# w2's last 96 rows as 32-row matmuls for eight token tiles at a time, in a fused attention and SwiGLU kernel

## The chip, the cores and the metric

The kernel runs on one core of one Trainium2 chip. The metric is the device time of one execution in microseconds, as the median of several runs. A core has the engines TensorE (matmuls, and a separate stream of weight loads), VectorE, ScalarE, GpSimd (called POOL in the profile) and SyncE (SP), which issues the transfers. The hardware profiler records one execution, instruction by instruction; that record is the trace, and its summary the profile.

## The reference

The input x has 2048 tokens of 512 elements (S = 2048, D = 512), all in bf16. The output mixes two branches token by token:

```
g = sigmoid(sum(x * gate_w))                # one number per token
a = linear_attention(x, wqkv) @ wo          # 32 heads of 16; phi(t) = elu(t) + 1 + 1e-6
b = (silu(x @ w1) * (x @ w3)) @ w2          # F = 1376 hidden columns
out = g * a + (1 - g) * b
```

In the attention, o = (phi(q) @ kv) / (phi(q) . z + 1e-6) with kv = sum over tokens of phi(k)^T v and z = sum of phi(k). There is no softmax, so kv, and its product with wo, are small matrices computed once.

F = 1376 is 10 x 128 + 96. The ten full slices of 128 hidden columns and the 96 that remain are handled apart; the change is about the 96.

## The kernel before

The tokens are 16 tiles of 128 (t), four tiles make a block (tb, 512 tokens). PSUM, where matmuls write, has eight banks of 128 x 512 fp32. The schedule is written out by hand: each engine runs its instructions in the order in which the program emits them, and all transfers of the main part go through SP's queue in order.

The first part (until about 47 us) loads x and the weights, projects q and k for each tile (L177), applies phi (L190 to L195), sums phi(k) on POOL (L209) and accumulates x^T phi(k) in banks 0 to 3 (L225).

The second part is a loop over the four blocks (L481). For each block, ten GLU steps (glu_step, L267) run: each makes a 128 x 512 piece of the hidden layer, already transposed (hidden columns on partitions, tokens along the row), with four matmuls for w1 (L272), four for w3 (L278), the silu on ScalarE (L283) and the product on VectorE (L284), into `hT[tb]`. These matmuls write banks 4 to 7 in rotation (`mm_tile`). In block 0, further steps stand between the GLU steps: kv_step after step 2 and m2_step after step 4 (L410, L426), which make the small attention matrix M2 with tiled matmuls (128 x 32 and 32 x 32 of the array), den_step (L316: the denominators on VectorE and POOL, the scaled q, and its transposing transfer to `pqT`), and rem_step.

rem_step(tb) (L231) handles the 96 remaining hidden columns and the gate for the four tiles of a block. Sixteen matmuls of 193 columns (L239: 96 of w1, 96 of w3, one of gate_w) give token-major results; silu, tanh and product follow (L245, L246, L249), the product goes into `hrem` (four tiles of 96 columns, padded to 128 with zeros that POOL wrote at the start, L92), `g_all` and `omg_all` get g and 1 - g (L254, L258), and a transposing transfer puts it behind the ten slices in `hT[tb][:, FC, :]` (L262).

After the ten GLU steps of a block, four output steps (out_step, L441) run, one for each tile. Each makes the attention part with four matmuls (L447), scales it by g on ScalarE into `aga` (L452), makes the GLU part with eleven matmuls, ten of 128 rows and one of 96 (L460), and on VectorE multiplies it by 1 - g, adds aga and writes `o` (L464), which is stored (L477). Both results use banks 0 to 3 in rotation (`ab_tile`). The last tile's GLU part is made in three column pieces (256, 128 and 128 columns), each of eleven matmuls. Between the output steps stand rem_step of the next block (after the second) and den_step for the next block's tiles (after each). The 96 rows of w2 are loaded by a transfer of their own, the last of the weight loads (L153).

Of the kernel before, what the change touches and what calls it, by code (L numbers as in the profile page):

```python
# [16 lines left out]
def kernel(  # L17
# [17 lines left out]
    nc = tc.nc  # L35
    P = nc.NUM_PARTITIONS

    Bb, S, D = A_x.shape
    F = B_w1.shape[1]
# [3 lines left out]
    NT = S // P  # L43
    TB = 512
    NTB = S // TB
    TPB = TB // P
    FC = F // P
    FR = F - FC * P
    F0 = FC * P
    HPC = P // Dh  # L50
    ZP = 4
    NR = 2 * FR + 1
    RP = 32
    RB = P // RP
    HPR = RP // Dh

    x2d = A_x.flatten_outer_dims()
    out2d = out.flatten_outer_dims()
# [5 lines left out]
    consts = ctx.enter_context(tc.tile_pool(name="consts", bufs=1))  # L64
    work = ctx.enter_context(tc.tile_pool(name="work", bufs=2))
# [12 lines left out]
        out=bmask[:], in_=bmask[:], pattern=[[-Dh, HPC], [0, Dh]], compare_op=ALU.is_ge,  # L78
# [15 lines left out]
    zaccb = consts.tile([P, D], BF16, name="zaccb")  # L94
    zb = consts.tile([P, D], BF16, name="zb")
# [18 lines left out]
    w2 = consts.tile([P, FC + 1, D], BF16, name="w2")  # L114
# [38 lines left out]
    dq.dma_start(out=w2[:FR, FC, :], in_=B_w2[F0:F, :])  # L153
# [76 lines left out]

    def rem_step(tb):  # L231

        hr = hrem[tb % 2]
        for half in range(2):
            ps = mm_tile()[:].rearrange("p (j n) -> p j n", j=2)
            for j in range(2):
                t = tb * TPB + half * 2 + j
                for kc in range(KC):
                    nc.tensor.matmul(  # L239
                        ps[:, j, 0:NR], lhsT=xT[:, kc, t * P : (t + 1) * P],  # L240
                        rhs=wr[:, kc, 0:NR], start=(kc == 0), stop=(kc == KC - 1),
                    )
# [3 lines left out]
            nc.scalar.activation(  # L246
                out=th_all[:, t0 : t0 + 2], in_=ps[:, :, 2 * FR], func=ACT.Tanh, scale=0.5
            )
            nc.vector.tensor_tensor(  # L249
                out=hr[:, half * 2 : half * 2 + 2, 0:FR], in0=ps[:, :, FR : 2 * FR],  # L250
                in1=sg[:], op=ALU.mult,
            )
# [5 lines left out]
        nc.vector.tensor_scalar(  # L258
            out=omg_all[:, tl], in0=th_all[:, tl], scalar1=-0.5, scalar2=0.5,
            op0=ALU.mult, op1=ALU.add,  # L260
        )
# [42 lines left out]
    def den_scale(t):  # L304
# [5 lines left out]
                :, :, :, :, None  # L310
            ].to_broadcast([P, KC, RB, HPR, Dh]),
            op=ALU.mult,
# [9 lines left out]


    hT = {}
    hT[0] = work.tile([P, FC + 1, TB], BF16, tag="hT", name="hT")
# [84 lines left out]
    def kv_step():  # L410
        kv_ps = ab_tile()[:, 0 : KC * RP].rearrange("p (c q) -> p c q", q=RP)
        for c in range(KC):
            for kc in range(KC):
                for g in range(RB):
                    fs = slice(c * P + g * RP, c * P + (g + 1) * RP)
                    nc.tensor.matmul(  # L416
# [9 lines left out]
    def m2_step():  # L426
        ps = [ab_tile() for _ in range(RB)]
        for c in range(KC):
            for g in range(RB):
                rows = slice(g * RP, (g + 1) * RP)  # L430
# [7 lines left out]
            else:  # L438
                nc.vector.tensor_copy(out=M2[:, g, :], in_=ps[g][:])

    def out_step(tb, tt):  # L441
        t = tb * TPB + tt
        ts = slice(t * P, (t + 1) * P)
        tl = slice(tt * P, (tt + 1) * P)
        a_ps = ab_tile()
        for c in range(KC):
            nc.tensor.matmul(  # L447
                a_ps[:], lhsT=pqT[:, c, ts], rhs=M2[:, c, :],
                start=(c == 0), stop=(c == KC - 1),
            )  # L450
        aga = work.tile([P, D], FP32, tag="aga", name="aga")
        nc.scalar.activation(out=aga[:], in_=a_ps[:], func=ACT.Copy, scale=g_all[:, t : t + 1])  # L452
        o = work.tile([P, D], BF16, tag="o", bufs=3, name="o")
        last = t == NT - 1
        for lo, w in ((0, 2 * P), (2 * P, P), (3 * P, P)) if last else ((0, D),):
            cs = slice(lo, lo + w)
            b_ps = ab_tile()
            for fc in range(FC + 1):
                n = P if fc < FC else FR
                nc.tensor.matmul(  # L460
                    b_ps[:, 0:w], lhsT=hT[tb][:n, fc, tl], rhs=w2[:n, fc, cs],
                    start=(fc == 0), stop=(fc == FC),
                )
            nc.vector.scalar_tensor_tensor(  # L464
                out=o[:, cs], in0=b_ps[:, 0:w], scalar=omg_all[:, t : t + 1], in1=aga[:, cs],
                op0=ALU.mult, op1=ALU.add,
            )
            if t < 2:
                rows = out2d[0 : 2 * P, :].rearrange("(p j) d -> p j d", j=2)[:, t, :]
            else:  # L470
                rows = out2d[ts, :]
            if last and w == P:

                if lo + w < D:
                    continue
                cs = slice(2 * P, D)
            dq.dma_start(out=rows[:, cs], in_=o[:, cs])  # L477

    z_step()
    den_at = {5: 0, 6: 1, 8: 2, 9: 3}  # L480
    for tb in range(NTB):  # L481
        for fc in range(FC):
            glu_step(tb, fc)
            if tb == 0:
                if fc in den_at:
                    den_step(den_at[fc])
                if fc == 2:
                    kv_step()
                if fc == 4:
                    m2_step()  # L490
                    z_order()
                    den_products(0)
                if fc == 7:
                    rem_step(0)
        for tt in range(TPB):
            out_step(tb, tt)
            if tb + 1 < NTB:
                if tt == 0:
                    hT[tb + 1] = work.tile([P, FC + 1, TB], BF16, tag="hT", name="hT")
# [33 lines left out]
```

## Time and profile before

| | |
|---|---|
| median of 3 runs | 178.66 us (178.36 to 179.07) |
| the profiled execution | 179.09 us, span 177.4 us |
| granted TensorE clock | 0.999 of full |
| TensorE matmuls, busy | 172.9 us, 97% of the span, 922 recorded |
| TensorE weight loads, busy | 83.5 us, 47% |
| VectorE, busy | 101.0 us, 57% |
| ScalarE, busy | 62.1 us, 35% |
| POOL, busy | 64.2 us, 36% |
| HBM read / written | 8.56 MB / 2.10 MB |

The span runs from the first to the last instruction of the profiled execution; its time is a little longer. In the profile, PE is TensorE's matmuls and PEld its weight loads, DVE is VectorE, ACT is ScalarE. A row of a group gives the line of the kernel, the engine, the operation, what is written and read, the shape and the count, then the busy time of the group in us, the mean duration of one in ns, and the idle time of the engine just before them with what ended it. A row of the timeline or of the chain gives the start and the length of a stretch in us. Matmuls overlap in their pipeline, so the busy time of a group isn't the count times the mean. Some records of matmuls can be missing, so a count can be short of the program's by a few.

### The profile page before, as it was taken

Reading aid. Unit: us, or ns where it says so; the run is one execution under the profiler, and the core shown is the slowest. Engines: PE = TensorE matmul, PEld = TensorE weight load, DVE = VectorE, ACT = ScalarE, POOL = GpSimd, SP = SyncE. Lnnn points to the kernel's source line nnn. Section 1 sums busy time; section 2 is a strip of 40 time slices with the busy share of each in tenths; the row PEclk is TensorE's granted clock in tenths of the full one; section 3 lists DMA queues with packets and bytes.
Section 4 is the critical chain, followed back from the end, with each engine's and each line's share of the span. In section 5 each row is a group of like instructions: output and inputs, shape, how many; then the busy total and the mean of one; then the engine's idle time right before and its main releaser. Section 6 shows DMA issues by size and latency. Waiting matters only on the chain.

```text
span 177.4 us, 2610 instructions
## 1 busy us (share of the span) xinstructions
PE 172.9 (97%) x922; PEld 83.5 (47%) x939; DVE 101.0 (57%) x195; ACT 62.1 (35%) x113; POOL 64.2 (36%) x108
## 2 busy tenths in 40 slices
PE   8999999999999999999999999999999999999993
PEld 5444444444444464644444464444445444444453
DVE  0299798888774988675434266634325664433222
ACT  3255444544644441332342223143322223342130
POOL 7077666567301867746200044540004432000000
PEclk9999999999999999999999999999999999999999
DMA  5998949994103022343100013510000332000001
GB/s 170 273 206 227 190 76 316 395 350 123 33 1 33 0 59 59 80 94 96 30 0 0 0 44 81 104 45 0 0 4 30 89 89 59 0 0 4 30 30 59
DMA packets 29724, 15.41 MB, mean 87 GB/s; under 512 B 21552, under 2 KB 28048, under 8 KB 29712
## 3 DMA queue, kind: packets, MB, share of 16 engines
q1 hardware_dynamic: 29440, 15.25, 34.3%
q8 instruction: 7, 0.11, 0.3%
q10 hardware_dynamic: 272, 0.01, 0.1%
q14 instruction: 5, 0.04, 0.1%
HBM read 8.56 MB, written 2.10 MB: 60 GB/s over the span
## 4 chain that ended last, share of the span: by engine, by line
PE 97%; issue 1%; DVE 0%
PE bank L460 21%; PE bank L278 20%; PE bank L272 19%; PE bank L177 16%; PE bank L225 8%; PE bank L447 8%; PE bank L239 3%; PE bank L328 2%; PE bank L334 1%; PE bank L416 0%; PE bank L431 0%; DVE o L464 0%
## 5 line engine op out<-in xcount | busy, mean ns | idle before, releaser
L284 DVE TENSOR_TENSOR hT<-bank,sg 128x512 bf16<-128x512 f32 x40 | 27.3, 682 | 32.4 <-PE bank L278 31.4
L278 PE MATMUL bank<-xT,w 128*128 128x512 bf16 x158 | 40.8, 379 | 0.2
L272 PE MATMUL bank<-xT,w 128*128 128x512 bf16 x156 | 40.5, 379 | 0.2
L460 PE MATMUL bank<-w,hT 128*128 128x512 bf16 (+3 forms) x194 | 40.5, 355 | 0.2
L283 ACT ACTIVATE sg<-bank 128x512 bf16<-128x512 f32 x40 | 23.9, 597 | 46.1 <-PE bank L272 43.8
L306 POOL TENSOR_TENSOR pqs<-pq,rden 128x512 bf16<-128x512 bf16 x16 | 16.9, 1057 | 55.1 <-issue 48.2
L177 PE MATMUL bank<-wqk,xT 128*128 128x512 bf16 x126 | 31.0, 387 | 0.1
L460 PEld LDWEIGHTS <-hT 128*128 128x128 bf16 (+1 forms) x198 | 18.5, 98 | 19.8
L209 POOL TENSOR_TENSOR zacc<-zacc,pk 128x128 f32<-128x128 f32 x56 | 23.3, 447 | 10.4 <-DVE pk L195 10.4
L464 DVE SCALAR_TENSOR_TENSOR o<-bank,omg_all,aga 128x512 bf16<-128x512 f32 (+2 forms) x18 | 12.4, 692 | 25.6 <-PE bank L460 25.5
L278 PEld LDWEIGHTS <-w 128*128 128x128 bf16 x160 | 15.6, 98 | 18.9
L272 PEld LDWEIGHTS <-w 128*128 128x128 bf16 x160 | 15.5, 98 | 18.5 <-issue 0.2
L452 ACT ACTIVATE aga<-bank,g_all 128x512 f32<-128x512 f32 x16 | 11.0, 687 | 28.9 <-PE bank L447 28.9
L177 PEld LDWEIGHTS <-xT 128*128 128x128 bf16 x128 | 12.7, 99 | 15.1 <-issue 0.6
L291 POOL TENSOR_TENSOR pr<-pq,zb 128x512 f32<-128x512 bf16 x16 | 18.5, 1156 | 0.1
L225 PE MATMUL bank<-pk,xN 128*128 128x512 bf16 x62 | 16.3, 379 | 0.2
L447 PE MATMUL bank<-M,pqT 128*128 128x512 bf16 x61 | 16.3, 378 | 0.2
L190 ACT ACTIVATE eq<-bank 128x512 bf16<-128x512 f32 x16 | 9.4, 598 | 16.0 <-PE bank L177 14.9
L195 DVE SCALAR_TENSOR_TENSOR pk<-bank,emk 128x512 bf16<-128x512 f32 x16 | 11.1, 691 | 1.6
L190 ACT ACTIVATE ek<-bank 128x512 bf16<-128x512 f32 x16 | 9.4, 597 | 7.2 <-PE bank L177 7.2
L195 DVE SCALAR_TENSOR_TENSOR pq<-bank,emq 128x512 bf16<-128x512 f32 x16 | 11.1, 692 | 0.5
L295 DVE TENSOR_REDUCE den<-pr 128x32 f32<-128x512 f32 x16 | 10.8, 676 | 0.0
(50 smaller groups left out, 81.3 us busy)
## 6 DMA issues: line engine op xcount, KB each, us to landing
w<-in_B_w_dram SPq DMA_DIRECT2D x3, 1280.0 KB, 10.5
out_dram<-o SPq DMA_DIRECT2D x15, 128.0 KB, 1.9
wqk<-in_A_wqkv_dram SPq DMA_DIRECT2D x4, 256.0 KB, 4.1
xN<-in_A_x_dram SPq DMA_DIRECT2D x1, 1024.0 KB, 5.6
xN<-in_A_x_dram SPq DMA_DIRECT2D x2, 256.0 KB, 3.1
xN<-in_A_x_dram SPq DMA_DIRECT2D x1, 512.0 KB, 4.2
wv<-in_A_wqkv_dram SPq DMA_DIRECT2D x1, 512.0 KB, 11.5
wo<-in_A_wo_dram SPq DMA_DIRECT2D x1, 512.0 KB, 12.4
```

Source lines behind the costliest of these rows:

```text
L177: nc.tensor.matmul(ps[:], lhsT=xT[:, kc, t * P : (t + 1) * P], rhs=w[:, kc, :], start=(kc == 0), stop=(kc == KC - 1),)
L190: nc.scalar.activation(out=e[:], in_=ps[:], func=ACT.Exp)
L195: nc.vector.scalar_tensor_tensor(out=dst, in0=ps[:], scalar=0.0, in1=em[:], op0=ALU.max, op1=ALU.add)
L209: nc.gpsimd.tensor_tensor(out=(zaccb if t == NT - 1 else zacc)[:, cs], in0=zacc[:, cs], in1=pk[t][:, cs], op=ALU.add,)
L225: nc.tensor.matmul(bank[kc][:], lhsT=xN[:, t, kc * P : (kc + 1) * P], rhs=pk[t][:], start=(t == 0), stop=(t == NT - 1),)
L272: nc.tensor.matmul(g_ps[:], lhsT=w1[:, kc, fs], rhs=xT[:, kc, tok], start=(kc == 0), stop=(kc == KC - 1),)
L278: nc.tensor.matmul(u_ps[:], lhsT=w3[:, kc, fs], rhs=xT[:, kc, tok], start=(kc == 0), stop=(kc == KC - 1),)
L283: nc.scalar.activation(out=sg[:], in_=g_ps[:], func=ACT.Silu)
L284: nc.vector.tensor_tensor(out=hT[tb][:, fc, :], in0=u_ps[:], in1=sg[:], op=ALU.mult)
L291: nc.gpsimd.tensor_tensor(out=pr[t][:], in0=pq[:, t, :], in1=zb[:], op=ALU.mult)
L447: nc.tensor.matmul(a_ps[:], lhsT=pqT[:, c, ts], rhs=M2[:, c, :], start=(c == 0), stop=(c == KC - 1),)
L460: nc.tensor.matmul(b_ps[:, 0:w], lhsT=hT[tb][:n, fc, tl], rhs=w2[:n, fc, cs], start=(fc == 0), stop=(fc == FC),)
```

## The change

The 96 remaining hidden columns are no longer the eleventh slice of `hT`. They are computed with the array divided into four groups of 32 rows, one for each tile of a block.

- rem_step writes its product into `hrow`, in the order slice r (3), tile j (4), row i (32), where hidden column 3i + r goes to row i of slice r. The transposing transfer (three 128 x 128 pieces instead of four) gives `hrT[tb % 2]`, in which partitions 32j to 32j + 31 hold tile j's 32 hidden rows of slice r. No zeros are needed, so the memsets go.
- w2's last 96 rows are loaded into `w2x` with the same regrouping, four times, once for each row group, by one transfer that reads the rows four times (384 KB written instead of 96).
- rem_out_step(tb, banks) makes, for the four tiles of a block, twelve matmuls of 32 rows, one for each r and j, with tile j's results in bank j of the four given.
- Two blocks are handled together, in the first output step of blocks 0 and 2 (out_first). It starts with three full matmuls of the first tile's GLU part (AHEAD), then runs rem_out_step for its own block into banks 0 to 3, where these sums stay for the block's four tiles, then rem_out_step for the next block into banks 4 to 7. rem_keep copies those four, multiplied by 1 - g, to SBUF (`rs`, two on ScalarE and two on VectorE). Then come the other seven matmuls of the first tile, and its attention part after them.
- In blocks 0 and 2, out_step's attention part uses banks 4 to 7 and its GLU part adds ten matmuls to what stands in banks 0 to 3. In blocks 1 and 3 (the kept ones), aga is made on VectorE, as g times the attention part plus `rs`, in place of ScalarE's scaling.
- rem_step(0) and rem_step(1) stand after the GLU steps 1 and 3 of block 0; rem_step(2) and rem_step(3) after the second and third output steps of block 1. Before, they stood after GLU step 7 of block 0 and after the second output step of blocks 0, 1 and 2.

```diff
+    RG = FR // RP
+    AHEAD = 3
...
-    hrem = [consts.tile([P, TPB, P], BF16, name=f"hrem{i}") for i in range(2)]
-    for h in hrem:
-        nc.gpsimd.memset(h[:], 0.0)
+    hrow = [consts.tile([P, RG, TPB, RP], BF16, name=f"hrow{i}") for i in range(2)]
+    hrT = [consts.tile([P, RG, P], BF16, name=f"hrT{i}") for i in range(2)]
+    w2x = consts.tile([P, RG, D], BF16, name="w2x")
...
-    dq.dma_start(out=w2[:, 0:FC, :], in_=w2_r)
-    dq.dma_start(out=w2[:FR, FC, :], in_=B_w2[F0:F, :])
+    dq.dma_start(out=w2[:], in_=w2_r)
+    w2x_r = B_w2[F0:F, :].rearrange("(i r) d -> i (r d)", i=RP)
+    dq.dma_start(
+        out=w2x[:].rearrange("p r d -> p (r d)"),
+        in_=w2x_r[None].to_broadcast([TPB, RP, RG * D]),
+    )
...
             nc.vector.tensor_tensor(
-                out=hr[:, half * 2 : half * 2 + 2, 0:FR], in0=ps[:, :, FR : 2 * FR],
-                in1=sg[:], op=ALU.mult,
+                out=hr[:, :, half * 2 : half * 2 + 2, :].rearrange("p r j i -> p j r i"),
+                in0=ps[:, :, FR : 2 * FR].rearrange("p j (i r) -> p j r i", i=RP),
+                in1=sg[:].rearrange("p j (i r) -> p j r i", i=RP), op=ALU.mult,
             )
...
         dq.dma_start(
-            out=hT[tb][:, FC, :].rearrange("p (tt q) -> p tt q", q=P),
-            in_=hr[:].rearrange("p tt f -> p (tt f)"), transpose=True,
-        )
+            out=hrT[tb % 2][:], in_=hr[:].rearrange("p r j i -> p (r j i)"), transpose=True,
+        )
+
+    def rem_out_step(tb, banks, started=(), ends=False):
+        for r in range(RG):
+            for j in range(TPB):
+                rows = slice(j * RP, (j + 1) * RP)
+                nc.tensor.matmul(
+                    banks[j][:], lhsT=hrT[tb % 2][rows, r, :], rhs=w2x[rows, r, :],
+                    start=(r == 0 and j not in started), stop=(ends and r == RG - 1),
+                )
+
+    rs = {}
+
+    def rem_keep(tb, banks):
+        for j in range(TPB):
+            t = tb * TPB + j
+            rs[t] = work.tile([P, D], FP32, tag="rs", bufs=TPB, name="rs")
+            omg = omg_all[:, t : t + 1]
+            if j % 2 == 0:
+                nc.scalar.activation(out=rs[t][:], in_=banks[j][:], func=ACT.Copy, scale=omg)
+            else:
+                nc.vector.tensor_scalar(
+                    out=rs[t][:], in0=banks[j][:], scalar1=omg, scalar2=None, op0=ALU.mult
+                )
...
+    def a_part(t, ps):
...
+        aga = work.tile([P, D], FP32, tag="aga", name="aga")
+        g = g_all[:, t : t + 1]
+        if t in rs:
+            nc.vector.scalar_tensor_tensor(
+                out=aga[:], in0=ps[:], scalar=g, in1=rs[t][:], op0=ALU.mult, op1=ALU.add
+            )
+        else:
+            nc.scalar.activation(out=aga[:], in_=ps[:], func=ACT.Copy, scale=g)
+        return aga
+
+    def b_part(t, ps, fcs, cs=slice(0, D), started=False):
+        tb, tt = divmod(t, TPB)
+        for fc in fcs:
+            nc.tensor.matmul(
+                ps[:, 0 : cs.stop - cs.start], lhsT=hT[tb][:, fc, tt * P : (tt + 1) * P],
+                rhs=w2[:, fc, cs], start=(fc == 0 and not started), stop=(fc == FC - 1),
+            )
...
+    def out_first(tb):
+        t = tb * TPB
+        b_part(t, bank[0], range(AHEAD))
+        rem_out_step(tb, bank, started=(0,))
+        keep = [mm_tile() for _ in range(TPB)]
+        rem_out_step(tb + 1, keep, ends=True)
+        rem_keep(tb + 1, keep)
+        b_part(t, bank[0], range(AHEAD, FC))
+        aga = a_part(t, mm_tile())
+        o = work.tile([P, D], BF16, tag="o", bufs=3, name="o")
+        mix(t, bank[0], aga, o)
+        store(t, o)
+
     def out_step(tb, tt):
         t = tb * TPB + tt
...
+        held = tb % 2 == 0
+        if held and tt == 0:
+            return out_first(tb)
+        aga = a_part(t, mm_tile() if held else ab_tile())
         o = work.tile([P, D], BF16, tag="o", bufs=3, name="o")
...
+        if t < NT - 1:
+            b_ps = bank[tt] if held else ab_tile()
+            b_part(t, b_ps, range(FC), started=held)
+            mix(t, b_ps, aga, o)
+            store(t, o)
+            return
...
+    rem_at = {1: 0, 3: 1}
...
-                if fc == 7:
-                    rem_step(0)
+                if fc in rem_at:
+                    rem_step(rem_at[fc])
         for tt in range(TPB):
             out_step(tb, tt)
             if tb + 1 < NTB:
...
-                if tt == 1:
-                    rem_step(tb + 1)
+                if tb == 1 and tt in (1, 2):
+                    rem_step(tb + tt)
                 den_step((tb + 1) * TPB + tt)
```

`mix` is the old L464 and `store` the old choice of rows with L477, as functions.

More of the change, by code (lines that the diff above doesn't have):

```diff
@@ L113 @@
     w3 = consts.tile([P, KC, F0], BF16, name="w3")
-    w2 = consts.tile([P, FC + 1, D], BF16, name="w2")
+    w2 = consts.tile([P, FC, D], BF16, name="w2")
     xT = consts.tile([P, KC, S], BF16, name="xT")
@@ L231, in rem_step @@
     def rem_step(tb):
-        hr = hrem[tb % 2]
+        hr = hrow[tb % 2]
         for half in range(2):
@@ L324 @@
     hT = {}
-    hT[0] = work.tile([P, FC + 1, TB], BF16, tag="hT", name="hT")
+    hT[0] = work.tile([P, FC, TB], BF16, tag="hT", name="hT")
     def warm_step(n):
@@ L451, in out_step @@
         aga = work.tile([P, D], FP32, tag="aga", name="aga")
-        nc.scalar.activation(out=aga[:], in_=a_ps[:], func=ACT.Copy, scale=g_all[:, t : t + 1])
-        o = work.tile([P, D], BF16, tag="o", bufs=3, name="o")
-        last = t == NT - 1
-        for lo, w in ((0, 2 * P), (2 * P, P), (3 * P, P)) if last else ((0, D),):
-            cs = slice(lo, lo + w)
-            b_ps = ab_tile()
[L458 to L462, printed above, removed]
-                )
[L464 to L477, printed above, removed]
@@ new lines, in mix, with store @@
+    def mix(t, ps, aga, o, cs=slice(0, D)):
+        nc.vector.scalar_tensor_tensor(
+            out=o[:, cs], in0=ps[:, 0 : cs.stop - cs.start], scalar=omg_all[:, t : t + 1],
+            in1=aga[:, cs], op0=ALU.mult, op1=ALU.add,
+        )
+    def store(t, o, cs=slice(0, D)):
+        if t < 2:
+            rows = out2d[0 : 2 * P, :].rearrange("(p j) d -> p j d", j=2)[:, t, :]
+        else:
+            rows = out2d[t * P : (t + 1) * P, :]
+        dq.dma_start(out=rows[:, cs], in_=o[:, cs])
@@ new lines, in out_first, with out_step @@
+    def out_first(tb):
[7 more added lines that the diff above has]
+        aga = a_part(t, mm_tile())
+        o = work.tile([P, D], BF16, tag="o", bufs=3, name="o")
+        mix(t, bank[0], aga, o)
+        store(t, o)
+    def out_step(tb, tt):
+        t = tb * TPB + tt
+        held = tb % 2 == 0
[9 more added lines that the diff above has]
+            return
+        for lo, hi in ((0, 2 * P), (2 * P, 3 * P), (3 * P, D)):
+            cs = slice(lo, hi)
+            b_ps = ab_tile()
+            b_part(t, b_ps, range(FC), cs)
+            mix(t, b_ps, aga, o, cs)
+            if lo == 0:
+                store(t, o, cs)
+        store(t, o, slice(2 * P, D))
@@ L498 @@
                 if tt == 0:
-                    hT[tb + 1] = work.tile([P, FC + 1, TB], BF16, tag="hT", name="hT")
-                if tt == 1:
-                    rem_step(tb + 1)
+                    hT[tb + 1] = work.tile([P, FC, TB], BF16, tag="hT", name="hT")
+                if tb == 1 and tt in (1, 2):
+                    rem_step(tb + tt)
                 den_step((tb + 1) * TPB + tt)
```

6 lines of the change are left out of this document (1 added, 5 removed).

## The prediction

> **What bounds the kernel now.** I read the page first: its busy shares, its row of granted clocks and its chain.
>
> ```profile
> span 177.4 us, 2610 instructions
> ...
> PE 172.9 (97%) x922; PEld 83.5 (47%) x939; DVE 101.0 (57%) x195; ACT 62.1 (35%) x113; POOL 64.2 (36%) x108
> ...
> PEclk9999999999999999999999999999999999999999
> ...
> PE 97%; issue 1%; DVE 0%
> ```
>
> TensorE is busy for 97% of the span at full granted clock, and the chain that ended last is TensorE for 97% too. No other engine passes 57%. So the change is worth what it takes from or adds to TensorE's own stream, unless it puts a hole into it. Then I read the chain in order of time for the price of a matmul, and the groups kept apart by shape (busy us, mean ns of one, idle before).
>
> ```profile
> 81.17 0.86 PE bank L272 x4
> 102.54 2.38 PE bank L460 x11
> 104.92 1.34 PE bank L239 x16
> 172.16 2.45 PE bank L460 x33
> ```
> ```profile
> L460 PE MATMUL bank<-w,hT 128*128 128x512 bf16 x146 | 34.4, 379 | 0.2
> L460 PEld LDWEIGHTS <-hT 128*128 128x128 bf16 x180 | 16.9, 98 | 18.0
> L460 PE MATMUL bank<-w,hT 96*128 96x512 bf16 x15 | 5.7, 381 | 0.1
> L416 PEld LDWEIGHTS <-wv 128*32 128x32 bf16 x64 | 0.6, 93 | 0.4 <-issue 0.4
> ```
>
> One matmul lasts 379 ns, but they overlap: a stage-two tile, eleven matmuls of 512 columns, advances the chain by 2.38 us, 0.216 us each. That holds with the 96-row one among them, so the 96-row matmul costs as much as a full one, 0.216 us. The last tile, in three column pieces, takes 2.45 us for 33. The 16 remainder matmuls of rem_step advance it by 1.34 us wherever they stand.
>
> **What is removed.** Fifteen 96-row matmuls of 512 columns, 15 x 0.216 = 3.24 us, and three in the last tile, a share of 3/33 of 2.45 us = 0.22 us. Sum 3.47 us, all on the path.
>
> **What is added on TensorE.** Two sessions (in out_first, token blocks 0 and 2). Each has 24 matmuls of 32 rows by 128 columns, moving 512: two blocks by three slices (r) of w2's last rows by four row groups (j). If the four of one r run together, a session is six rounds. The trace of before has no 32x128 tile; the nearest rows are the two tiled stretches it has, kv_step (64 matmuls 128*32, moving 32) and m2_step (16 matmuls 32*32, moving 512).
>
> ```profile
> 51.26 1.03 PE L278 MATMUL bank<-xT,w 128*128 128x512 bf16 x4
> 52.21 0.56 PEld L416 LDWEIGHTS <-wv 128*32 128x32 bf16 x64 [0.42 <-issue]
> 52.21 0.66 PE L416 MATMUL bank<-Gsb,wv 128*32 128x32 bf16 x64
> ...
> 53.68 1.03 PE L278 MATMUL bank<-xT,w 128*128 128x512 bf16 x4
> ...
> 55.41 1.03 PE L278 MATMUL bank<-xT,w 128*128 128x512 bf16 x4
> 56.36 0.14 PEld L431 LDWEIGHTS <-kvT 32*32 32x32 bf16 x16 [0.42 <-issue]
> 56.36 0.43 PE L431 MATMUL bank<-wo,kvT 32*32 32x512 bf16 x16
> ...
> 57.60 1.03 PE L278 MATMUL bank<-xT,w 128*128 128x512 bf16 x4
> ```
>
> m2_step stands between two L278 groups whose starts are 57.60 - 55.41 = 2.19 us apart; two untiled groups of four are 2 x 0.865 = 1.73, so m2_step costs 0.46 us. Its 16 matmuls are all in flight within 0.43 us, four row groups into four banks at once, each bank over all its 128 partitions: the same output traffic that a round of four 32x128 tiles makes. So the concurrency is shown, and one round costs 0.216 us of streaming plus 0.245 us for changing to tiles and back. kv_step costs 53.68 - 51.26 - 1.73 = 0.69 us for 16 rounds on the same four column groups. Less one change (0.245) that is 0.445 / 16 = 28 ns a round, weight loads included, though one load alone lasts 93 ns (0.56 us of load time hold 64 of them, and the 16 of m2_step overlap in 0.14 us). So in tiled mode, too, loads run ahead beneath the matmuls before them. Scaled by columns (128 against 32), a round's loads need 4 x 28 = 112 ns, less than the 216 ns of streaming, and are hidden.
>
> A session is then 0.46 + 5 x 0.216 = 1.54 us, two are 3.08 us. Bounds: with a free change 6 x 0.216 = 1.30 us each, 2.60 in all; with every round paying load, fill and drain anew as m2_step's single one does, 6 x 0.46 = 2.76 each, 5.52 in all. I take 3.08, because kv_step's rounds are repeated ones like these and m2_step's single one is not.
>
> Whether a load runs ahead beneath matmuls on its own row groups is seen untiled at the border of two blocks (start, us, engine):
>
> ```profile
> 97.41 1.03 PE L278 MATMUL bank<-xT,w 128*128 128x512 bf16 x4
> 97.61 0.60 ACT L283 ACTIVATE sg<-bank 128x512 bf16<-128x512 f32 x1 [1.13 <-PE bank L272]
> 98.06 0.75 PEld L447 LDWEIGHTS <-pqT 128*128 128x128 bf16 x4
> 98.27 1.03 PE L447 MATMUL bank<-M,pqT 128*128 128x512 bf16 x4
> 98.54 0.69 DVE L284 TENSOR_TENSOR hT<-bank,sg 128x512 bf16<-128x512 f32 x1 [1.04 <-PE bank L278]
> ```
>
> L447's first load starts at 98.06, while the last L278 matmul (started 97.41 + 3 x 0.216 = 98.06) uses every row group. So loads do overlap matmuls on their own rows here; the other reading is kept as rival 1, at 179.25 us.
>
> A rule of the Trainium skill (TensorE: Matmul & The Clock Gate, Part 3: Packing small matmuls — row/col tiling) is the one of rival 1: a weight load overlaps matmuls in flight only where the row group differs, and in a session each round loads the row groups that the round before still uses. The row at 98.06 differs from it. The same section gives a measured 3.07x for four row tiles of this shape, by which (an estimate from that page) 24 x 0.216 / 3.07 makes 1.69 us a session and 178.6 us in all.
>
> **Waits on TensorE.** out_first starts with three full matmuls (0.65 us), then block tb's session (0.65 + change), then block tb+1's into the four banks 4 to 7 that the last two GLU steps used. In these rows the last GLU matmul of the block ends its slot at 98.27 and VectorE frees the last of the four banks at 98.54 + 0.69 = 99.23, 0.96 us later; the second half reaches it after 0.65 + 0.65 + 0.1 = 1.4 us. No wait, 0.4 us to spare. The copies of rem_keep, two on ScalarE and two on VectorE, are priced by
>
> ```profile
> L452 ACT ACTIVATE aga<-bank,g_all 128x512 f32<-128x512 f32 x16 | 11.0, 687 | 28.9 <-PE bank L447 28.9
> L406 DVE CAST Gsb<-bank 128x512 bf16<-128x512 f32 x2 | 1.3, 680 | 0.0
> ```
>
> as 0.69 us each: the first pair ends some 0.9 us after the session, the second at 1.6. The next to need those banks is a_part after seven full matmuls (1.51 us): bank by bank, 0.87 us or more apart. Covered; uncovered it would be at most 0.9 us per session. In out_first a_part now stands after b_part, so aga and the mix come later by about 1.8 us, and den_step and the store queue behind them on VectorE, POOL and SP. Their reader is the next block, over 17 us on (the GLU steps). Bank 0's next writer is too.
>
> **VectorE in the odd blocks.** There aga moves from ScalarE to VectorE (the ScalarE work falls off at no gain), and rem_step for blocks 2 and 3 both stand in block 1.
>
> ```profile
> L464 DVE SCALAR_TENSOR_TENSOR o<-bank,omg_all,aga 128x512 bf16<-128x512 f32 x3 | 2.3, 751 | 5.0 <-PE bank L460 5.0
> L295 DVE TENSOR_REDUCE den<-pr 128x32 f32<-128x512 f32 x3 | 2.0, 677 | 0.0
> L302 DVE RECIPROCAL rden<-den 128x32 f32<-128x32 f32 x3 | 1.1, 353 | 0.1
> L249 DVE TENSOR_TENSOR hrem<-bank,sgr 128x192 bf16<-128x192 f32 x2 | 0.7, 358 | 0.6 <-ACT th_all L246 0.6
> ...
> L298 DVE TENSOR_SCALAR den<-den 128x32 f32<-128x32 f32 x3 | 0.5, 181 | 0.1
> L258 DVE TENSOR_SCALAR omg_all<-th_all 128x4 f32<-128x4 f32 x1 | 0.2, 161 | 0.0
> ```
>
> A step costs VectorE 2 x 0.75 + 0.68 + 0.35 + 0.18 = 2.71 us against TensorE's 14 x 0.216 = 3.03; with a rem_step, 2 x 0.36 + 2 x 0.16 = 1.04 more against 1.34. Following the queue through block 1, the second and third steps' aga waits behind den_step, and VectorE enters block 2 about 0.5 us late. The GLU banks allow two steps' grace (1.73 us between a step's matmuls and their bank's next use), so TensorE doesn't wait. A longer product in rem_step (its reads now step by three; between 0.36 us and the 0.69 of a full 128x512 one) leaves that so. In the last block nothing but aga and mix is left; the end keeps its order, mix of 0.35 and store.
>
> **Loads and queues.** SP carries as many transfers as before.
>
> ```profile
> 33.58 4.12 SPq L153 DMA_DIRECT2D w<-in_B_w_dram  x1
> 46.94 1.19 SPq L390 DMA_TRANSPOSE zaT<-zaccb  x1
> ```
> ```profile
> w<-in_B_w_dram SPq DMA_DIRECT2D x1, 96.0 KB, 10.1
> hT<-hrem SPq DMA_TRANSPOSE x4, 2.4
> ```
>
> The four-fold load of w2's last rows moves 384 KB in place of 96, at the same place in the queue. The old one landed at 33.58 + 10.1 = 43.7 us. Even a load twice as long lands by 53.8, before its first use at about 69; zaT goes out at 46.94 and can meet the extra 288 KB, but the z chain behind it has slack since rem_step(0) and (1) now stand before the first den_step. The hrT transposes (2.4 us) have six GLU steps (6 x 1.73 = 10.4 us) in block 0, and all ten before block 2. The hrem memsets on POOL vanish beside idle time. All of it: 0.
>
> **Sum.** -3.47 + 3.08 = -0.39 us. The profiled execution took 179.09 us (span 177.4, 1.69 around it) and would take 178.7; it is 0.43 above the median of the runs, 178.66, which becomes 178.3.
>
> **The rivals.**
> (1) Weight loads don't run ahead in row tiles. Each of the ten repeated rounds then shows one 98 ns load: +0.98 us on the forecast, 179.25. Speaking for it is the skill's rule above; the rows at 98.06 and kv_step's 28 ns rounds speak against it.
> (2) Slower: rounds don't follow one another freely, because the four 128-column loads of a round go one after another (4 x 98 = 392 ns a round, 180.0 us) or because each round fills and drains (460 ns, 180.7 us). It decides for slower by 0.5% when a repeated round passes 0.345 us: (3.47 + 0.9) / 2 - 0.46, divided by 5. For it: no trace row shows 128-column loads in row groups; against it: 33 untiled loads and matmuls fit into 2.45 us in the last tile, 74 ns each, so loads don't need 98 ns of their own.
> (3) A new wait: the second half of a session on VectorE's release of bank 7, or block 1's late VectorE. 0.4 us to spare there, over a microsecond here; price up to 0.9 us a place, about 179.7.
> (4) The four matmuls don't run together at all: 24 x 0.216 + 0.245 = 5.43 us a session, +7.4 us, 186.1. m2_step's row excludes it nearly.
> (5) The change of tile mode is free: 2.60 us for both sessions, 177.8. That is the most the change can give (0.87 us, 0.49%).
>
> **How the numbers follow.** Forecast 0.66, (1) 0.12, (2) 0.12, (3) 0.04, (4) 0.02, (5) 0.04. A difference below 0.5% (0.9 us) is about what a measurement of this kernel can tell from none. Faster by more: (5) with some scatter and a little of the forecast, 0.07. Slower: (2), (3), (4) and a sixth of (1), 0.20. The rest, 0.73, is within. The likeliest case alone spans 178.0 to 178.7. The range takes in (5) with 0.1 us of scatter, 177.7, and (1) and the cheaper half of (2), 180.1; outside lie (4), the dearer half of (2) and the tails.
>
> **What would show it.** In the trace after: the 24 matmuls of hrT as one stretch of about 1.5 us, twice, each round 0.216 us after the last; (1) gives 0.31 us a round, (2) 0.39 or more; TensorE with no idle before a_part or the keep banks; the b_part stream of ten at 2.16 us; the span near 177.0. It goes wrong if the change of mode with 128-column weights costs more than m2_step's, or if a round's loads wait for its predecessor.

## The result and the profile after

The changed kernel takes 178.38 us (median of 22 runs, 177.85 to 178.78) against 178.76 us for the kernel before in as many; the ratio is 0.9973, 95% interval 0.9962 to 0.9983. In a second comparison of 12 runs (after2 below) it is 0.9970 (0.9952 to 0.9989). That is 0.4 to 0.5 us less, inside the 0.5% that the prediction counts as no difference, but clear of zero.

The page of the changed kernel, and its chain in order of time (start, us, engine, count) around the first output step of block 0 and at the end. In this kernel L278 is rem_out_step, L303 and L309 are the GLU matmuls, L475 the attention part, L492 the GLU part of an output tile:

```profile
span 176.3 us, 2685 instructions
...
PE 172.5 (98%) x969; PEld 82.5 (47%) x969; DVE 110.4 (63%) x207; ACT 59.1 (34%) x109; POOL 63.2 (36%) x106
```
```profile
68.27 1.41 PE bank L278 x24
69.68 1.62 PE bank L492 x7
71.30 1.73 PE bank L475 x8
73.02 2.16 PE bank L492 x10
...
171.31 2.22 PE bank L492 x30
```

TensorE is still the bound, at 98%. An output tile's GLU part is 2.16 us in place of 2.38, the last tile's 2.22 in place of 2.45. The new work is 24 matmuls in one stretch, twice. Its price is best read from the timeline, where the change of mode falls between the rows:

```profile
67.46 0.81 PE L492 MATMUL bank<-w,hT 128*128 128x512 bf16 x3
68.20 0.98 PEld L278 LDWEIGHTS <-hrT 32*128 32x128 bf16 x24 [0.42 <-issue]
68.21 1.47 PE L278 MATMUL bank<-w2x,hrT 32*128 32x512 bf16 x24
69.61 1.69 PE L492 MATMUL bank<-w,hT 128*128 128x512 bf16 x7
...
71.13 1.89 PE L475 MATMUL bank<-M,pqT 128*128 128x512 bf16 x8
```

From 67.46 to 71.13 are 3.67 us, of which ten full matmuls take 2.16: a session costs 1.51 us (in block 2, 134.02 - 130.35 - 2.16, the same). Six rounds of 0.216 are 1.30, so the change of mode and back costs 0.21.

The stretch from the first GLU matmul to the end of the last matmul shows the sum. Before, it went from 46.94 to 172.16 + 2.45 = 174.61, 127.67 us; here from

```profile
46.36 1.03 PE L303 MATMUL bank<-xT,w 128*128 128x512 bf16 x4
```

to 171.31 + 2.22 = 173.53, 127.17 us: 0.50 less. The two spans differ by 1.1 us, but the other 0.6 lie ahead of that stretch, where the first loads arrive: over the traces of all these kernels, the first GLU matmul started between 46.3 and 47.5 us.

The work around it on the other engines (busy us, mean ns of one, idle before):

```profile
L482 DVE SCALAR_TENSOR_TENSOR aga<-bank,g_all,rs 128x512 f32<-128x512 f32 x8 | 5.7, 714 | 0.5
L255 DVE TENSOR_TENSOR hrow<-bank,sgr 128x192 bf16<-128x192 f32 x8 | 2.9, 358 | 2.5 <-ACT th_all L252 2.5
L294 DVE TENSOR_SCALAR rs<-bank,omg_all 128x512 f32<-128x512 f32 x4 | 2.7, 722 | 1.3 <-PE bank L278 1.3
L292 ACT ACTIVATE rs<-bank,omg_all 128x512 f32<-128x512 f32 x4 | 2.5, 684 | 4.6 <-PE bank L278 4.6
```

VectorE's busy time rises from 101.0 to 110.4 us (mostly eight aga and four copies); TensorE waits for none of it. The product with reads that step by three takes 358 ns, as before.

### The profile page after: what moved, and what is told of

Same layout as the page of the kernel before. It is cut to its first block, busy times and chain, and to the rows that moved or that the text cites. A ratio compares the mean times of both kernels' runs of the same rounds, so it can differ in the third digit from the quotient of the medians.

```text
span 176.3 us, 2685 instructions
## 1 busy us (share of the span) xinstructions
PE 172.5 (98%) x969; PEld 82.5 (47%) x969; DVE 110.4 (63%) x207; ACT 59.1 (34%) x109; POOL 63.2 (36%) x106
## 4 chain that ended last, share of the span: by engine, by line
PE 94%; DMA 2%; SPq 1%; DVE 0%; issue 0%
PE bank L492 20%; PE bank L303 20%; PE bank L309 20%; PE bank L183 15%; PE bank L231 8%; PE bank L475 8%; PE bank L245 3%; DMA wqk<-in_A_wqkv_dram 2%; PE bank L278 2%; SPq L126 1%; PE bank L447 0%; SPq L129 0%; PE bank L462 0%; DVE o L498 0%
## 5 line engine op out<-in xcount | busy, mean ns | idle before, releaser
L303 PE MATMUL bank<-xT,w 128*128 128x512 bf16 x160 | 41.1, 379 | 0.0
L309 PE MATMUL bank<-xT,w 128*128 128x512 bf16 x160 | 41.1, 379 | 0.0
L492 PE MATMUL bank<-w,hT 128*128 128x512 bf16 (+2 forms) x180 | 37.5, 355 | 0.0
L492 PEld LDWEIGHTS <-hT 128*128 128x128 bf16 x180 | 16.7, 98 | 18.4 <-issue 0.8
L309 PEld LDWEIGHTS <-w 128*128 128x128 bf16 x160 | 15.7, 98 | 18.9
L303 PEld LDWEIGHTS <-w 128*128 128x128 bf16 x160 | 15.5, 98 | 18.2 <-issue 0.2
L475 PE MATMUL bank<-M,pqT 128*128 128x512 bf16 x64 | 16.1, 379 | 0.0
L231 PEld LDWEIGHTS <-xN 128*128 128x128 bf16 x64 | 6.3, 98 | 7.6
## 6 DMA issues: line engine op xcount, KB each, us to landing
wv<-in_A_wqkv_dram SPq DMA_DIRECT2D x1, 512.0 KB, 11.2
```

What stands on the lines that cost most here:

```text
L231: nc.tensor.matmul(bank[kc][:], lhsT=xN[:, t, kc * P : (kc + 1) * P], rhs=pk[t][:], start=(t == 0), stop=(t == NT - 1),)
L303: nc.tensor.matmul(g_ps[:], lhsT=w1[:, kc, fs], rhs=xT[:, kc, tok], start=(kc == 0), stop=(kc == KC - 1),)
L309: nc.tensor.matmul(u_ps[:], lhsT=w3[:, kc, fs], rhs=xT[:, kc, tok], start=(kc == 0), stop=(kc == KC - 1),)
L475: nc.tensor.matmul(ps[:], lhsT=pqT[:, c, ts], rhs=M2[:, c, :], start=(c == 0), stop=(c == KC - 1),)
L492: nc.tensor.matmul(ps[:, 0 : cs.stop - cs.start], lhsT=hT[tb][:, fc, tt * P : (tt + 1) * P], rhs=w2[:, fc, cs], start=(fc == 0 and not sta ...
```

## The experiments

Times are compared with the kernel before on the same chip; lengths of a session are read from the timeline as above. The changed kernel's own are 178.38 us and 1.51 us. A slot is 0.216 us, the time that one matmul of 512 columns takes in a row of them. Small differences of medians have to be read with care: a median less the stretch from the first GLU matmul to the end of the last (as traced in one execution) is 51.1 us for the kernel before, 51.2 for the changed one, 51.4 and 51.2 for the two runs of moves and 51.4 for four. So some 0.3 us between the medians of two programs can lie outside that stretch, and below 0.5 us the lengths in the traces decide.

**One more change of mode: split.**

```diff
         rem_out_step(tb, bank, started=(0,))
+        b_part(t, bank[0], range(AHEAD, 2 * AHEAD), started=True)
         keep = [mm_tile() for _ in range(TPB)]
...
-        b_part(t, bank[0], range(AHEAD, FC))
+        b_part(t, bank[0], range(2 * AHEAD, FC))
```

> Three more full matmuls of the first tile stand between the two halves of a session, so TensorE changes to row tiles twice in a visit instead of once; the matmuls are the same. Theory (a change to tiles and back costs 0.21 us, each round 0.216 us, loads hidden): + 2 x 0.21 = 0.42 us against the changed kernel, 178.8 us, and each half 0.65 + 0.21 = 0.86 us. Rival (the change is free and every round pays 0.251 us, 1.51 / 6, because its loads show): no difference, each half 0.75 us.

Measured: 178.72 us, ratio 0.9994 (0.9979 to 1.0010), 0.34 us above the changed kernel. In the timeline:

```profile
68.07 0.81 PE L492 MATMUL bank<-w,hT 128*128 128x512 bf16 x3
68.81 0.83 PE L278 MATMUL bank<-w2x,hrT 32*128 32x512 bf16 x12
69.57 0.82 PE L492 MATMUL bank<-w,hT 128*128 128x512 bf16 x3
70.33 0.83 PE L278 MATMUL bank<-w2x,hrT 32*128 32x512 bf16 x12
71.08 1.04 PE L492 MATMUL bank<-w,hT 128*128 128x512 bf16 x4
71.96 1.89 PE L475 MATMUL bank<-M,pqT 128*128 128x512 bf16 x8
```

71.96 - 68.07 - 2.16 = 1.73 us: 0.22 more than in one session, with the same 24 matmuls. So the change is what costs 0.21 to 0.22 us, and the rounds are not dearer than 0.216.

**Twice the rounds: twice.**

```diff
-        for r in range(RG):
+        for k in range(2 * RG):
+            r = k % RG
...
-                    start=(r == 0 and j not in started), stop=(ends and r == RG - 1),
+                    start=(k == 0 and j not in started), stop=(ends and k == 2 * RG - 1),
```

> Every block's twelve 32-row matmuls are made twice, so the 96 hidden columns count twice in the output; twelve rounds in a session in place of six, one change of mode as before. Theory: a session of 0.21 + 12 x 0.216 = 2.81 us, + 2 x 1.30 = 2.60 us against the changed kernel, 181.0 us. Rival with loads showing: 12 x 0.251 = 3.02 us a session, + 3.02 us, 181.4 us. Rival with a full restart in each round (0.46 us): + 5.5 us.

Measured: 181.18 us, ratio 1.0142 (1.0116 to 1.0168); 2.80 us above the changed kernel. The timeline has the session between

```profile
68.58 0.81 PE L493 MATMUL bank<-w,hT 128*128 128x512 bf16 x3
69.32 2.77 PE L279 MATMUL bank<-w2x,hrT 32*128 32x512 bf16 x48
72.02 1.68 PE L493 MATMUL bank<-w,hT 128*128 128x512 bf16 x7
73.54 1.89 PE L476 MATMUL bank<-M,pqT 128*128 128x512 bf16 x8
```

so that it costs 73.54 - 68.58 - 2.16 = 2.80 us: 1.29 more for six more rounds, 0.215 each, weight loads included. The loads of a round are hidden beneath the round before, on the same row groups. Two such sessions make 2.58 us; the other 0.2 of the 2.80 between the medians is within the scatter named above. With split, the price of a session of n rounds is settled: 0.21 + n x 0.216 us.

**No concurrency: onegroup.**

```diff
-                rows = slice(j * RP, (j + 1) * RP)
+                rows = slice(0, RP)
```

> All 24 matmuls of a session use row group 0, so every tile of a block gets tile 0's hidden rows. Theory (a 32-row matmul costs what a full one does, and only four row groups together pay): 24 x 0.216 + 0.21 = 5.40 us a session, + 7.8 us against the changed kernel, 186.2 us. Rival (a 32-row matmul on its own is cheaper than a full one, by rows): clearly less than that.

Measured: 189.55 us, ratio 1.0632 (1.0593 to 1.0672), 11.2 us above the changed kernel, 3.4 more than the theory gave. The sessions are as long as it said:

```profile
67.90 0.81 PE L492 MATMUL bank<-w,hT 128*128 128x512 bf16 x3
68.64 5.35 PE L278 MATMUL bank<-w2x,hrT 32*128 32x512 bf16 x24
73.92 3.17 PE L492 MATMUL bank<-w,hT 128*128 128x512 bf16 x7
76.89 2.11 PE L475 MATMUL bank<-M,pqT 128*128 128x512 bf16 x8
```

73.92 - 67.90 - 0.65 = 5.37 us: a 32-row matmul by itself costs what a full one does. But the seven full matmuls behind it take 76.89 - 73.92 = 2.97 us instead of 1.51. A table by stretches (us from and to, length, busy us and count for PE, PEld, DVE, ACT and POOL, then the granted clock, the share of the transfers and GB/s) says why:

```profile
68.64:73.90 5.26, 5.26 (x25) 2.14 (x24) 2.75 (x5) 0.52 (x1) 4.25 (x4) 1.00 0.22 45
73.90:77.00 3.10, 3.10 (x9) 1.12 (x9) 1.11 (x2) 0.75 (x2) 0.00 (x0) 0.50 0.10 20
77.00:80.00 3.00, 3.00 (x15) 1.30 (x14) 1.11 (x2) 1.37 (x2) 0.00 (x0) 0.95 0.00 0
```

After five microseconds with one row group of four at work, the clock was granted at half speed for some 3 us. It happens after both sessions. The seven matmuls take 1.46 us longer than usual and the attention part behind them some 0.2, so it costs about 1.7 us each: the 3.4 us.

**Half the array for the same time: twogroups.** The edit of twice, and

```diff
-                rows = slice(j * RP, (j + 1) * RP)
+                rows = slice(j % 2 * RP, (j % 2 + 1) * RP)
```

> Each block's twelve matmuls are made twice, on row groups 0 and 1 only, so the 96 hidden columns count twice and tiles 2 and 3 get the rows of 0 and 1. 48 matmuls on two groups are 24 slots, the same 5.2 us as with one group. Theory A (the clock was granted at half speed after the one-group session because three quarters of the array stood idle; half the array is still too little): 5.40 us a session and some 1.6 us of slow matmuls behind each, 189.5 us. Theory B (half the array is enough): 5.40 us a session, no slow stretch, 178.4 + 7.8 = 186.2 us.

Measured: 186.18 us, ratio 1.0419 (1.0397 to 1.0441). Theory B to 0.02 us: the session is as long, nothing behind it is slow, and the mean granted clock of the profiled execution is 1.000, against 0.982 in onegroup.

```profile
68.77 5.35 PE L279 MATMUL bank<-w2x,hrT 32*128 32x512 bf16 x48
74.05 1.68 PE L493 MATMUL bank<-w,hT 128*128 128x512 bf16 x7
75.57 1.89 PE L476 MATMUL bank<-M,pqT 128*128 128x512 bf16 x8
```

So tiles as such don't bring the clock down. For stretches of this length one row group of four does and two don't. The two runs differ in the rows at work and in the matmuls per time alike, and which of them counts isn't shown.

**The order within a session: jfirst.**

```diff
-        for r in range(RG):
-            for j in range(TPB):
+        for j in range(TPB):
+            for r in range(RG):
```

> Only the order of the twelve matmuls changes: all three slices of one row group, then the next row group. Theory (TensorE starts matmuls in program order, and only neighbours on different row groups run together): 24 matmuls less 7 places where the row group changes are 17 slots of 0.216 us, 3.68 + 0.21 = 3.89 us a session, + 4.8 us against the changed kernel, 183.1 us. Rival (the sequencer finds the free row groups further down its queue): no difference, 178.4 us.

Measured: 178.66 us, ratio 0.9994 (0.9974 to 1.0014), and in the timeline a session of 71.22 - 67.53 - 2.16 = 1.53 us:

```profile
67.53 0.81 PE L492 MATMUL bank<-w,hT 128*128 128x512 bf16 x3
68.27 1.49 PE L278 MATMUL bank<-w2x,hrT 32*128 32x512 bf16 x24
69.70 1.69 PE L492 MATMUL bank<-w,hT 128*128 128x512 bf16 x7
71.22 1.89 PE L475 MATMUL bank<-M,pqT 128*128 128x512 bf16 x8
```

The theory fell. With 17 slots one after another the stretch would be 3.68 us long; it is 1.49. TensorE doesn't start matmuls strictly in program order: those of a free row group pass those that wait for a busy one. The trace doesn't say which tile a matmul belongs to, but in jall and jdeep below the emitted order does cost time, which speaks against a reordering ahead of the chip. The median is 0.28 us above the changed kernel's and the intervals overlap; the sessions differ by 0.02 us each.

**How far it looks: jall and jdeep.** In jall the 24 matmuls are ordered by row group over both blocks, six of a group in a row; jdeep makes each twice (REP = 2), twelve in a row.

```diff
+        for j in range(TPB):
+            rows = slice(j * RP, (j + 1) * RP)
+            for b, banks in ((tb, bank), (tb + 1, keep)):
...
+                for k in range(REP * RG):
+                    r = k % RG
+                    nc.tensor.matmul(
+                        banks[j][:], lhsT=hrT[b % 2][rows, r, :], rhs=w2x[rows, r, :],
...
```

> A session's 24 matmuls ordered by row group: the six of group 0 (both blocks), then the six of group 1, and so on. Group 3's first load stands 36 instructions behind the session's first. Theory (each row group runs its own next matmul as long as the sequencer sees it, and it sees at least that far): a session of 1.51 us as in the changed kernel. Rival (it sees only the some 18 instructions that the earlier reordering needed): group 3 starts about 9 slots late, a session of about 3.4 us.

> The same order with every matmul made twice (the 96 hidden columns count twice): twelve matmuls a group, group 3's first load 72 instructions behind the first. With a view of 72 or more instructions: 0.21 + 12 x 0.216 = 2.80 us a session. With a shorter view each pair of load and matmul that is missing delays group 3 by one slot of 0.216 us: a view of 64 gives 3.7 us, one of 36 gives 6.7 us at most (5.2 us are 24 slots).

Both were run once. jall took 180.61 us:

```profile
67.39 0.81 PE L498 MATMUL bank<-w,hT 128*128 128x512 bf16 x3
...
68.13 2.82 PE L283 MATMUL bank<-w2x,hrT 32*128 32x512 bf16 x24
...
69.63 0.69 ACT L298 ACTIVATE rs<-bank,omg_all 128x512 f32<-128x512 f32 x1 [2.31 <-PE bank L283]
...
70.53 0.69 ACT L298 ACTIVATE rs<-bank,omg_all 128x512 f32<-128x512 f32 x1 [0.21 <-PE bank L283]
...
70.88 1.68 PE L498 MATMUL bank<-w,hT 128*128 128x512 bf16 x7
...
72.40 1.89 PE L481 MATMUL bank<-M,pqT 128*128 128x512 bf16 x8
```

Its session is 72.40 - 67.39 - 2.16 = 2.85 us, twelve slots and the change of mode, between both expectations. The two ScalarE rows are the copies of banks 4 and 6, which row groups 0 and 2 fill, and both wait for TensorE. The second starts 0.90 us after the first, so group 2 ran four slots behind group 0: two slots for each step from one row group to the next.

jdeep took 201.07 us, with the clock at half speed from about 73.2 us on. The first two copies, and the stretches (clock last but two):

```profile
71.02 0.69 ACT L298 ACTIVATE rs<-bank,omg_all 128x512 f32<-128x512 f32 x1 [3.61 <-PE bank L283]
...
72.76 0.75 DVE L300 TENSOR_SCALAR rs<-bank,omg_all 128x512 f32<-128x512 f32 x1 [2.02 <-PE bank L283]
```
```profile
68.20:73.20 5.00, 5.00 (x32) 2.27 (x32) 2.90 (x5) 0.69 (x1) 4.27 (x4) 0.99 0.17 35
73.20:76.60 3.40, 3.40 (x13) 1.21 (x12) 0.31 (x1) 0.69 (x1) 0.00 (x0) 0.50 0.18 36
```

Its session lasted from 68.2 to 79.0 us, some 23 slots at full and 13 at half speed, 36 in all. That is 7.8 us at full clock, beyond every one of its expectations. Here the copy of bank 5 (row group 1) starts 1.74 us after that of bank 4 (row group 0), eight slots.

So a view that reaches a fixed number of instructions ahead doesn't fit, but one simple rule fits all three orders: the next row group starts when no more than three matmuls of the group before it are still to start. With six in a row that is 6 - 4 = 2 slots later, and the session is 6 + 3 x 2 = 12 slots; with twelve it is 12 - 4 = 8 slots, and 12 + 3 x 8 = 36; with three (jfirst) there is no delay. The rule was found from these runs and not tested by another.

jdeep also says more on the clock: 31 of its matmuls started in the first 5.0 us (23 slots), 1.3 row groups at work on average, and the clock fell; with two at work throughout (twogroups) it didn't.

**A session for each block: four.**

```diff
+        last = tb == NTB - 1
+        b_ps = ab_tile() if last else bank[0]
+        b_part(t, b_ps, range(AHEAD))
+        if last:
+            keep = [mm_tile() for _ in range(TPB)]
+            rem_out_step(tb, keep, ends=True)
+            rem_keep(tb, keep)
+        else:
+            rem_out_step(tb, bank, started=(0,))
+        b_part(t, b_ps, range(AHEAD, FC))
...
-        held = tb % 2 == 0
-        if held and tt == 0:
+        held = tb < NTB - 1
+        if tt == 0:
             return out_first(tb)
```

> Every block makes its own session of twelve matmuls (three rounds) at its first output step; blocks 0, 1 and 2 hold the sums in banks 0 to 3, and only block 3 copies them out, so VectorE's aga with rs stands in block 3 alone. Theory (0.21 us for each change of mode, on the path): four sessions of 0.65 + 0.21 = 0.86 us, and in block 3 about 0.2 us of waiting for bank 7, 3.6 us in all against 3.0 in the changed kernel: + 0.6 us, 179.0 us, about the kernel before. Rival (pairing two blocks buys nothing): 178.4 us.

Measured: 179.28 us, ratio 1.0030 (1.0015 to 1.0045), slower than the kernel before. The sessions cost 0.87, 0.87, 0.86 and 1.11 us, 3.71 in all, 0.69 more than the two of the changed kernel. The last, 164.18 - 160.91 - 2.16, waits some 0.24 us for bank 7:

```profile
160.91 0.81 PE L492 MATMUL bank<-w,hT 128*128 128x512 bf16 x3
...
164.18 1.89 PE L475 MATMUL bank<-M,pqT 128*128 128x512 bf16 x8
```

The stretch from the first GLU matmul (46.48) to the end of the last (172.11 + 2.22) is 127.85 us, 0.68 longer than in the changed kernel and 0.18 longer than before. Without pairing, row tiles win nothing: two more changes of mode and one wait use up what the shared rounds save.

**Nothing ahead of the session: ahead0.**

```diff
-    AHEAD = 3
+    AHEAD = 0
...
-        b_part(t, bank[0], range(AHEAD))
-        rem_out_step(tb, bank, started=(0,))
+        rem_out_step(tb, bank)
...
-        b_part(t, bank[0], range(AHEAD, FC))
+        b_part(t, bank[0], range(AHEAD, FC), started=True)
```

> The three full matmuls ahead of a session go behind it. Theory (the second half needs bank 7, which VectorE frees 1.14 us after the last GLU matmul's slot in block 0 and 0.96 us after it in block 2, and reaches it after 0.65 + 0.1 = 0.75 us): sessions longer by 0.4 and 0.2 us, + 0.6 us against the changed kernel, 179.0 us. Rival (the sequencer does other row groups' matmuls meanwhile and hides it): 178.4 us.

Measured: 178.93 us, ratio 1.0016 (0.9997 to 1.0035), 0.55 us above the changed kernel. The wait is in the loads' row of block 0, in two parts, the second behind VectorE's release of bank 7 (hT, 68.49 + 0.63):

```profile
68.07 0.55 PEld L278 LDWEIGHTS <-hrT 32*128 32x128 bf16 x16 [0.42 <-issue]
68.07 1.90 PE L278 MATMUL bank<-w2x,hrT 32*128 32x512 bf16 x24
...
68.49 0.63 DVE L315 TENSOR_TENSOR hT<-bank,sg 128x512 bf16<-128x512 f32 x1
...
69.17 0.30 PEld L278 LDWEIGHTS <-hrT 32*128 32x128 bf16 x8 [0.55 <-issue]
```

The sessions, counted from the end of the last GLU slot, cost 1.94 and 1.76 us, 0.43 and 0.25 more, as expected. The rival fell with it: the wait isn't hidden by the other row groups' matmuls. The three matmuls ahead hide that wait; without them the gain is gone.

**The moves alone: moves and moves2.** The kernel before with rem_step at its new places, and `bufs=NTB` for hT:

```diff
...
-                if fc == 7:
-                    rem_step(0)
+                if fc in rem_at:
+                    rem_step(rem_at[fc])
...
-                if tt == 1:
-                    rem_step(tb + 1)
+                if tb == 1 and tt in (1, 2):
+                    rem_step(tb + tt)
```

> The kernel before with rem_step alone moved to the places of the changed kernel (blocks 0 and 1 after GLU steps 1 and 3, blocks 2 and 3 in block 1's output steps), its eleventh slice and 96-row matmuls as they were, hT with four buffers so that the early transfers have a place. Theory (rem_step takes 1.34 us of TensorE wherever it stands): no difference to the kernel before, 178.8 us. Rival (part of the gain comes from the new places): 178.4 to 178.6 us.

> The kernel with rem_step alone moved, once more, beside the changed kernel on one chip. Theory: within 0.1 us of the kernel before, since its TensorE stream from the first GLU step on had the same length. Rival (the new places cost 0.3 us, which the sessions have to win back first): 179.1 us again, ratio 1.0018.

Measured: 179.10 us and 178.94 us, ratio 1.0018 both times (1.0004 to 1.0033 and 1.0000 to 1.0036). So the moves give nothing of the gain. The stretch from the first GLU matmul to the end of the last is 127.67 us (46.56 to 171.78 + 2.45) and 127.70 us (46.78 to 172.02 + 2.46), the same as before (127.67), so what makes 0.3 us between the medians isn't in this stretch in the executions that were traced. It is no more than other programs differ by outside the stretch, and the changed kernel, which has the moves too, shows 0.1 us there; what it is, is open.

**The changed kernel beside moves2: after2.** No edit.

> The changed kernel once more, beside moves2 on one chip. Theory (two sessions of 1.51 us for 3.47 us of 96-row matmuls, nothing else): - 0.46 us against the kernel before, ratio 0.9974. If the moves cost 0.3 us: ratio 0.9990.

Measured: 178.11 us, ratio 0.9970 (0.9952 to 0.9989). The kernel with the moves alone stood at 178.94 on the same chip. The theory's number holds; the 0.9990 of the other lies just outside the interval.

## Why the prediction was right

The forecast was 178.3 us and the median is 178.38, 0.38 us less than before where the sum said 0.39. That the two agree to 0.01 us is luck in part: the interval of the measured difference is 0.4 us wide, and the forecast started from a median of 3 runs. In the traces two terms were off by some 0.06 us each, the same way, so the stretch is 0.50 us shorter. The mechanism held. By its steps:

- **The bound.** TensorE's stream decides before and after, at 97% and 98% busy. All experiments moved the time, to within 0.5 us, by what they added to that stream.
- **Removed, 3.47 us.** The rows after give 15 x (2.38 - 2.16) + 2.45 - 2.22 = 3.53 us in rounded figures, 0.06 more than forecast.
- **Added, 3.08 us.** 2 x 1.51 = 3.02 us, 0.06 less than forecast. The change of mode, priced from m2_step as 0.245 us, is 0.21 (after) to 0.22 (split); the rounds are 0.215 (twice). The stretch comes out 0.50 us shorter, against 0.39. That m2_step and kv_step would price a shape that the trace didn't have was the step most open to doubt, and it held. The estimate of 112 ns for a round's loads isn't far off either: the 24 loads of the first session keep the load stream busy for 0.54 us, 0.09 a round.
- **Rival 1, loads that don't run ahead,** is excluded by twice: 0.215 us a round, where it needed 0.31. The Trainium skill's rule in TensorE: Matmul & The Clock Gate (Part 3: Packing small matmuls — row/col tiling), that loads overlap only where the row group differs, doesn't hold in these traces. Its 3.07x is 24 x 0.216 / 1.51 = 3.4x here with the change of mode counted.
- **Rival 2, rounds that don't follow freely,** needed more than 0.345 us a round; excluded by the same run.
- **Rival 3, a new wait.** None in the changed kernel, but the cover is real: ahead0 shows the wait for bank 7 as 0.43 and 0.25 us, and four shows one of 0.24 in block 3, whose session goes straight to the banks that the GLU steps used. The prediction took 0.96 us for the release in both blocks. In block 0 it is 1.14, since VectorE has den_step in hand; 0.3 us to spare, not 0.4. Block 1's VectorE was to enter block 2 about 0.5 us late; its first product there starts at 115.15, 0.34 us after the slot of the matmuls that it waits for (113.95 + 0.86), where the last product of block 0 starts 0.51 after its own (67.97 against 67.46), and 0.27 is what the prediction's rows show (98.54 against 98.27). So VectorE came into block 2 less than 0.1 us late, not 0.5. In the changed kernel's timeline:

```profile
67.97 0.63 DVE L315 TENSOR_TENSOR hT<-bank,sg 128x512 bf16<-128x512 f32 x1
...
113.95 1.03 PE L309 MATMUL bank<-xT,w 128*128 128x512 bf16 x4
...
115.15 0.63 DVE L315 TENSOR_TENSOR hT<-bank,sg 128x512 bf16<-128x512 f32 x1
```
- **Rival 4, no concurrency,** would have been worse than priced: 189.6 us instead of 186.1, as the clock falls as well. **Rival 5, a free change of mode,** is excluded by split.
- **Waits and moves at no cost.** Loads, transposes, copies and VectorE's aga cost TensorE nothing in the stretch. For the moves this holds too; the 0.3 us between the medians of moves and of the kernel before is unexplained. If the changed kernel paid it as well, the sessions would win more than the stretch shows; the traces don't show that.

## What to carry to other kernels

A contraction remainder of 96 rows costs a full matmul; as 32-row tiles, four at a time, it costs three quarters, plus 0.21 us for each change of mode to tiles and back, so gather enough rounds behind one change (here six; with three a session was no gain). Put full matmuls ahead of a tiled stretch until the banks that it needs are free, and in one that lasts some 5 us keep at least two of the four row groups at work. Order its matmuls so that the row groups alternate, or put at most three of a group in a row. The price of a tiled stretch could be read ahead of time here from the other tiled stretches in the trace, of other shapes: the distance between the untiled groups around it, less what these take.

## What the hardware showed that was not expected

- Matmuls in row tiles pass one another: ordered group by group, 24 of them take 1.49 us (jfirst), where program order would make 3.68; with six in a row for each group (jall) the session goes to 2.85 us, and with twelve (jdeep) to 36 slots. All three lengths fit a next row group that starts when no more than three matmuls of the group before it are still to start. The Trainium skill (TensorE: Matmul & The Clock Gate, Part 3: Packing small matmuls — row/col tiling) says that matmuls start and end strictly in program order; these lengths don't agree with it.
- A quarter of the array at work for 5.4 us brought the granted clock to 0.50 for some 3 us afterwards (onegroup), half of it did not (twogroups, 186.18 us against 189.55), and 1.3 row groups on average did (jdeep, 0.50 from about 73.2 us on). The Trainium skill (TensorE: Matmul & The Clock Gate, Part 1: The HAM clock gate) has a half and a full rate and a window of 3.4 us; the rows fit both.
